# One K tile and one V tile of a cached attention step, loaded in three parts of 56, 64 and 8 partitions

## The chip, the cores and the metric

The kernel runs on one NeuronCore of a Trainium2 chip. The metric is the device time of one execution in microseconds (us). Profiles are of one execution, taken by the hardware profiler. The engines are called PE (TensorE, matmuls), PEld (its weight loads), DVE (VectorE), ACT (ScalarE), POOL (GpSimd) and SP (SyncE, which here only issues transfers). Transfers run on the core's 16 DMA engines, which are not in this list.

## The reference

One decode step of a transformer block for two sequences (B = 2, one new token each, D = 512), with 32 query heads, 8 K/V heads of 128 elements, and a cache of 32768 positions. All is float32. Cut to what matters:

```python
xn = layernorm(x)
q = (xn @ wq)                                   # 32 heads of 128
scores = einsum("bhqd,bhkd->bhqk", q, k) * 128 ** -0.5   # 4 query heads share a K/V head
o = einsum("bhqk,bhkd->bhqd", softmax(scores), v)
s = o.reshape(B, 1, 4096) @ wo
gate, up = xn @ W_gate, xn @ W_up
g = silu(((gate * (gate > 0)) * up) @ W_down)
out = x + s * g
```

The two caches are 2 x 8 x 32768 x 128 x 4 bytes = 268 MB each, and every byte is read once. The sum over positions in softmax and in the weighted sum of V doesn't depend on the order of the positions, as long as K and V are taken in the same order.

## The kernel before

The work is cut into 16 groups g, one for each sequence and K/V head, and each group into NU = 8 tiles of 4096 positions (`TK`). So there are 128 K tiles and 128 V tiles, numbered t = 0 to 127; tile t belongs to group t // 8. A tile is 2 MB: 128 partitions by 4096 floats, that is, each partition holds one row of 16 KB, which is 32 successive positions. `load_tile` makes one transfer of it, `rows` in device memory to `flat` in the tile, 128 rows of 16 KB (only V's last tile comes in two halves of the columns). All loads are issued on SP's queue, by `load`, in program order. Small loads of x (two rows each) are issued on ACT's queue at the start.

All big tiles live in one ring of `SLOTS = 8` buffers ("r"). A load can be issued when the buffer's last user is done: for a K tile that is the second of its two transposes on VectorE (`k_transpose`, line 298), for a V tile the last of its eight matmuls (`values`, line 383).

The main loop goes over steps s. In step s:

- VectorE transposes K tile s in 32 x 32 blocks, in two halves, into `kts` (line 298);
- PE multiplies it with the queries into `s` (`scores`, line 308), 16 matmuls;
- VectorE takes the scores of step s - 1 out of PSUM with their maximum (line 322);
- eight steps later, when the group's maximum is known, ACT has made the exponentials (line 359), PE and VectorE turn them (lines 365 and 374), and PE multiplies V tile v = s - 9 (`OFF = NU + LAG`) with them into `o_ps` (line 383).

When a group is done, its output is scaled and turned (`take_o`, `finish_group`), and after each K/V head PE multiplies with that head's rows of wo (`project_o`, line 434). The last head's wo rows (two transfers) are the last loads of the program, behind the two halves of the last V tile; the last matmuls on them, the product with the gate and the sum with x (lines 444 and 445) and two small stores (line 551) end the program. The MLP is done in the first steps.

Loads are issued `DEPTH = 3` steps ahead of their use: after step s, the table `ahead` has K tile s + 3 and V tile s + 3 - 9. So in steady state K and V loads alternate on SP, and tile k_64 and tile v_64 are 18 tiles apart in this order.

A load's completion is told by a semaphore. Loads take eight such semaphores (DMAHW0 to DMAHW7 in what follows) in turn, so a load uses the semaphore of the load eight issues before it and has to know that one landed.

Of the kernel before, what the change touches and what calls it, by code (L numbers as in the profile page):

```python
# [21 lines left out]
SLOTS = 8  # L22
DEPTH = 3
ALIGN = 512


@with_exitstack
def kernel(
# [18 lines left out]
    NU = SK // TK  # L47
    NG = B * HKV
# [34 lines left out]
    n = 1  # L83
# [41 lines left out]
    def load(dst, src):  # L125
        nc.sync.dma_start(dst, src)

    def group(g):
        return g % B, g // B

    def load_tile(dst, src, t, pieces):
        b, hk = group(t // NU)
        lo = (t % NU) * TK
        rows = src[b, hk, lo : lo + TK, :].rearrange("(p r) d -> p (r d)", p=P)
        flat = dst.rearrange("p c j d -> p (c j d)")
        c = 0
        for n in pieces:
            part = slice(c * NJ * DH, (c + n) * NJ * DH)
            load(flat[:, part], rows[:, part])
            c += n  # L140

    def load_k(t):
        KT[t] = ring.tile([P, NC, NJ, DH], F32, tag="r", align_bytes=ALIGN, name=f"k_{t}")
        load_tile(KT[t], kc, t, (NC,))

    def load_v(t):
        VT[t] = ring.tile([P, NC, NJ, DH], F32, tag="r", align_bytes=ALIGN, name=f"v_{t}")
        load_tile(VT[t], vc, t, (NC,) if t < NG * NU - 1 else LAST)

    def load_wo(hk):  # L150
        WO[hk] = ring.tile([P, 2, 2, D], F32, tag="r", align_bytes=ALIGN, name=f"wo_{hk}")
        r = REP * DH
        dst = WO[hk].rearrange("p c i d -> p c (i d)")
        rows = wo[hk * r : (hk + 1) * r, :].rearrange("(c p i) d -> p c (i d)", c=2, i=2)
        if hk < HKV - 1:
            load(dst, rows)
        else:
            for c in range(2):
                load(dst[:, c], rows[:, c])
# [5 lines left out]
    def load_wq(k):  # L165
        wqt[k] = ring.tile([P, 2, QW], F32, tag="r", align_bytes=ALIGN, name=f"wq_{k}")
        load(wqt[k].rearrange("p h n -> p (h n)"), wq[k * P : (k + 1) * P, :])
# [60 lines left out]
    def load_gu(which, half):  # L228
        t = ring.tile([P, 2, F], F32, tag="r", align_bytes=ALIGN, name=f"w{which}_{half}")
        w = wg if which == "g" else wu  # L230
        load(
            t.rearrange("p k f -> p (k f)"),
            w[half * 2 * P : (half + 1) * 2 * P, :].rearrange("(p k) f -> p (k f)", k=2),
        )
        for k in range(2):
            mlp[which, half * 2 + k] = t[:, k, :]
# [31 lines left out]
    def load_d(half):  # L268
        t = ring.tile([P, FH, D], F32, tag="r", align_bytes=ALIGN, name=f"wd_{half}")
        load(  # L270
            t.rearrange("p i d -> p (i d)"),
            wd.rearrange("(p i) d -> p (i d)", p=P)[:, half * FH * D : (half + 1) * FH * D],
        )
        for i in range(FH):
            mlp["d", half * FH + i] = t[:, i, :]
# [273 lines left out]
    rows = res.rearrange("(c q) n -> q c n", q=32)  # L549
# [33 lines left out]
```

## Time and profile before

| | |
|---|---|
| median of 3 runs | 1330.6 us (1330.4 to 1331.05) |
| the profiled execution | 1330.78 us |
| its span in the profile | 1328.9 us |
| DMA engines (queue q1, all loads of SP) | 99.5% of 16 engines' span, 564.68 MB |
| PE / DVE / ACT busy | 66% / 55% / 5% |
| a K load, from issue to landing | 28.4 us (median) |
| mean rate over the span | 426 GB/s |

The span is from the first to the last instruction of the profile; the profiled execution's time is 1.9 us longer. A DMA share is the mean share of time in which the 16 DMA engines had a packet in hand. Packets are the rows that a transfer moves (16 KB for a tile's row) and small ones of 4 bytes that close a transfer on an engine. "K from issue to landing" covers the wait in the engines' queues, since several loads are in flight at a time.

### The profile page before, as it was taken

To read this page: it belongs to the slowest core of one execution; us is meant where nothing else is said; L and a number is where in the kernel's file an instruction comes from. 1 tells how busy PE (TensorE), PEld (TensorE's weight loads), DVE (VectorE), ACT (ScalarE), POOL (GpSimd) and SP (SyncE) were. 2 spreads that over 40 slices of the span, in tenths; PEclk is the share of its full clock that TensorE was granted. 3 is DMA by queue.
4 is the path that set the end of the run, shared out by engine and by line. 5 is a ranking of instruction groups with operands and counts; after the bars stand their busy time and mean duration, and the time that the engine had idled before them with its cause. 6 is when DMAs were issued, how large, how long until landed. Compare 5 with 4: busy or idle time off the path is not lost.

```text
span 1328.9 us, 17052 instructions
## 1 busy us (share of the span) xinstructions
PE 872.7 (66%) x7544; PEld 338.5 (25%) x7544; DVE 727.7 (55%) x976; ACT 69.1 (5%) x261; POOL 0.7 (0%) x6
## 2 busy tenths in 40 slices
PE   4566675676666658566676766667676675767676
PEld 1232232232223223232222322223222231222222
DVE  5775555555645555554555555545555554646541
ACT  0001010100101000010100101000010100101010
POOL 0000000000000000000000000000000000000000
PEclk9778877888788887888887778878887787788888
DMA  9999999999999999999999999999999999999996
GB/s 397 430 430 431 430 429 431 430 430 430 430 431 429 431 431 430 429 430 431 429 431 428 431 431 430 431 429 431 431 428 431 429 431 431 429 431 430 431 431 288
DMA packets 40749, 565.77 MB, mean 426 GB/s; under 512 B 4434, under 2 KB 4450, under 8 KB 6500
## 3 DMA queue, kind: packets, MB, share of 16 engines
q1 hardware_dynamic: 40648, 564.68, 99.5%
q8 instruction: 59, 0.97, 0.3%
q14 instruction: 14, 0.11, 0.0%
q10 hardware_dynamic: 28, 0.01, 0.0%
HBM read 564.67 MB, written 0.00 MB: 425 GB/s over the span
## 4 chain that ended last, share of the span: by engine, by line
DMA 74%; DVE 14%; PE 11%; issue 0%; DVEq 0%
DMA k<-in_A_k_cache_dram 68%; DVE kts L298 12%; PE s L308 5%; PE o_ps L383 4%; DMA v<-in_A_v_cache_dram 2%; DMA wo<-in_A_wo_dram 2%; DMA wq<-in_A_wq_dram 2%; DVE sc L322 1%; PE pt L365 0%; DVE qt L220 0%; PE ps_u L242 0%; PE ps_d L281 0%; DVE os L406 0%; PE pq L198 0%; DVE boot L212 0%
## 5 line engine op out<-in xcount | busy, mean ns | idle before, releaser
L298 DVE STREAM_TRANSPOSE kts<-k 128x2048 f32<-128x2048 f32 x256 | 590.4, 2307 | 459.6 <-DMA k<-in_A_k_cache_dram 459.6
L308 PE MATMUL s<-kts,qt 128*32 128x256 f32 x4096 | 455.1, 526 | 326.5 <-DVE kts L298 322.5
L383 PE MATMUL o_ps<-v,sc 128*16 128x512 f32 (+1 forms) x2064 | 343.0, 685 | 6.2 <-DMA v<-in_A_v_cache_dram 6.1
L308 PEld LDWEIGHTS s<-kts,qt 128*32 128x32 f32 x4096 | 173.8, 141 | 556.5 <-issue 278.3
L383 PEld LDWEIGHTS o_ps<-v,sc 128*16 128x16 f32 (+1 forms) x2064 | 91.4, 115 | 149.6 <-issue 136.4
L359 ACT ACTIVATE sc<-sc,nb 128x256 f32<-128x256 f32 x128 | 63.2, 496 | 1126.4 <-DVE nb L355 1126.4
L374 DVE STREAM_TRANSPOSE sc<-pt 128x256 f32<-128x256 f32 x128 | 53.1, 415 | 82.4 <-PE pt L365 82.3
L365 PE MATMUL pt<-sc,perm 128*128 128x256 f32 x256 | 94.5, 453 | 0.9 <-ACT sc L359 0.9
L365 PEld LDWEIGHTS pt<-sc,perm 128*128 128x128 f32 x256 | 40.6, 199 | 112.4 <-issue 100.0
L322 DVE TENSOR_SCALAR_CACHE_REDUCE sc<-s 128x256 f32<-128x256 f32 x128 | 50.1, 392 | 5.9 <-PE s L308 5.5
L416 PE MATMUL po<-sel,os 128*64 128x4 f32 x512 | 25.0, 209 | 14.3 <-DVE os L406 14.3
L351 PE MATMUL pr<-negone,mrow 1*128 1x1 f32 x32 | 8.9, 344 | 37.5 <-DVE mrow L348 37.5
L336 PE MATMUL pr<-ident,m 128*1 128x128 f32 x16 | 4.6, 289 | 40.2 <-DVE m L334 40.2
L416 PEld LDWEIGHTS po<-sel,os 128*64 128x64 f32 x512 | 23.6, 147 | 20.8 <-DVE os L406 20.8
L359 ACT ACTIVATION_READ_ACCUMULATOR sc<-sc,nb 128x1 f32 x128 | 24.1, 188 | 0.0
L351 PEld LDWEIGHTS pr<-negone,mrow 1*128 1x128 f32 x32 | 7.5, 291 | 40.8 <-DVE mrow L348 40.8
L406 DVE TENSOR_SCALAR os<-o_ps,rl 128x512 f32<-128x512 f32 x16 | 12.0, 751 | 9.7 <-PE o_ps L383 8.5
L336 PEld LDWEIGHTS pr<-ident,m 128*1 128x1 f32 x16 | 1.3, 79 | 54.5 <-DVE m L334 53.6
L434 PE MATMUL py<-wo,ots 128*32 128x128 f32 x256 | 12.6, 313 | 0.1
L399 PE MATMUL pl<-l,same 128*128 128x1 f32 x32 | 6.7, 280 | 8.8 <-DVE l L397 8.8
L198 PE MATMUL pq<-wq,xnt 128*32 128x512 f32 x64 | 9.8, 769 | 2.7 <-DMA wq<-in_A_wq_dram 2.3
L434 PEld LDWEIGHTS py<-wo,ots 128*32 128x32 f32 x256 | 10.5, 131 | 2.0 <-issue 0.9
(69 smaller groups left out, 112.1 us busy)
## 6 DMA issues: line engine op xcount, KB each, us to landing
k<-in_A_k_cache_dram SPq DMA_DIRECT2D x128, 2048.0 KB, 28.4
v<-in_A_v_cache_dram SPq DMA_DIRECT2D x127, 2048.0 KB, 29.0
wq<-in_A_wq_dram SPq DMA_DIRECT2D x4, 2048.0 KB, 13.3
wo<-in_A_wo_dram SPq DMA_DIRECT2D x7, 1024.0 KB, 27.2
wg<-in_B_W_gate_dram SPq DMA_DIRECT2D x2, 1792.0 KB
wu<-in_B_W_up_dram SPq DMA_DIRECT2D x2, 1792.0 KB, 33.9
wd<-in_B_W_down_dram SPq DMA_DIRECT2D x2, 1792.0 KB
v<-in_A_v_cache_dram SPq DMA_DIRECT2D x2, 1024.0 KB
```

The lines of the kernel that those rows point to most:

```text
L198: nc.tensor.matmul(pq[half][32 * c : 32 * c + 32, :], xnt[:, k, :], wqt[k][:, half, c * 512 : (c + 1) * 512], start=(k == 0), stop=(k == N ...
L298: nc.vector.transpose(KTS[t][:, i * half : (i + 1) * half], src[:, i * half : (i + 1) * half])
L308: nc.tensor.matmul(ps[Q * c : Q * c + Q, :], qt[:, b, hk, e, :], mov[:, e, c], start=(e == 0), stop=(e == 3),)
L322: nc.vector.tensor_scalar(ST[t].rearrange("p j m -> p (j m)"), SPS.pop(t), SCALE, None, op0=ALU.mult, op1=ALU.max, accum_out=MX[g][:, u : ...
L351: nc.tensor.matmul(pr[:, 256:257], mrow.rearrange("o c k h -> o (c k h)"), negone, start=True, stop=True)
L359: nc.scalar.activation(st, st, AF.Exp, bias=nbias, scale=1.0, accum_out=LS[g][:, u : u + 1])
L365: nc.tensor.matmul(PW[t], perm.rearrange("p k c h -> p (k c h)"), ST[t].rearrange("p j m -> p (j m)"), start=True, stop=True,)
L374: nc.vector.transpose(ST[t].rearrange("p j m -> p (j m)"), PW.pop(t))
L383: nc.tensor.matmul(ops[g % 2][a : a + n * REP, :n, :], w[:, j, c * REP : (c + n) * REP], v[:, c : c + n, j, :], start=(u == 0 and j < 4), ...
L406: nc.vector.tensor_scalar(OS[g], ops[g % 2], rl, None, op0=ALU.mult)
L416: nc.tensor.matmul(pr[64 * r : 64 * r + 64, i * REP : (i + 1) * REP], o2[:, c, i, :], sel[:, c, :], start=(c == 0), stop=(c == NC - 1),)
L434: nc.tensor.matmul(py[32 * c : 32 * c + 32, :P], ots[:, hk % 2, k // 2, k % 2, :], w[:, k // 2, k % 2, c * P : (c + 1) * P], start=(hk == ...
```

## The change

Where tile t is 64 (`NG * NU // 2`), for K and for V, `load_tile` makes three transfers instead of one, of partitions 0 to 55, 56 to 119 and 120 to 127. In the first, the 56 source rows are taken as a 7 x 8 array, `(q a) -> a q` with a = 7: the seven values of a are the outer dimension, and partition 8a + q gets source row 7q + a. The other two keep the order of rows. The K tile and the V tile are permuted alike.

```diff
+PARTS = ((56, 7), (64, 0), (8, 0))
...
         flat = dst.rearrange("p c j d -> p (c j d)")
+        if t == NG * NU // 2:
+            p = 0
+            for n, a in PARTS:
+                part = rows[p : p + n, :]
+                load(flat[p : p + n, :], part.rearrange("(q a) f -> a q f", a=a) if a else part)
+                p += n
+            return
         c = 0
         for n in pieces:
```

In the built program four transfers more stand on SP's queue; the instructions of the other engines are the same. The place of k_64 on SP's queue, before (a row is the line, the operation, the tile and its source, partitions by elements, and what the issue waits for; PE_49 and DVE_49 are the semaphores of these engines, the number behind a tile's name is the buffer's):

```order
L126 DMA v_55_3013<-in_A_v_cache_dram 128x4096 [waits DMAHW2_49,DMAHW1_49,DVE_49]
L126 DMA k_64_3015<-in_A_k_cache_dram 128x4096 [waits PE_49]
L126 DMA v_56_3050<-in_A_v_cache_dram 128x4096 [waits DMAHW4_49,DMAHW3_49,DVE_49]
L126 DMA k_65_3052<-in_A_k_cache_dram 128x4096 [waits PE_49]
L126 DMA v_57_3087<-in_A_v_cache_dram 128x4096 [waits DMAHW6_49,DMAHW5_49,DVE_49]
```

Before, a V load's wait on two semaphores covers itself and the K load behind it. The same place after the change:

```order
L127 DMA v_55_3013<-in_A_v_cache_dram 128x4096 [waits DMAHW2_49,DMAHW1_49,DVE_49]
L127 DMA k_64_3015<-in_A_k_cache_dram 56x1x4096 [waits PE_49]
L127 DMA k_64_3015<-in_A_k_cache_dram 64x4096 [waits DMAHW3_49]
L127 DMA k_64_3015<-in_A_k_cache_dram 8x4096 [waits DMAHW4_49]
L127 DMA v_56_3052<-in_A_v_cache_dram 128x4096 [waits DMAHW5_49,DVE_49]
L127 DMA k_65_3054<-in_A_k_cache_dram 128x4096 [waits DMAHW6_49,PE_49]
L127 DMA v_57_3089<-in_A_v_cache_dram 128x4096 [waits DMAHW7_49,DVE_49]
```

The second and the third part wait for a semaphore of their own, and so does each of the next loads, up to k_67; since the tile took three semaphores, "eight issues before" is there the tile six places before instead of eight. The place of v_64 on SP's queue, before:

```order
L126 DMA wo_3_3363<-in_A_wo_dram 128x2x1024 [waits DMAHW4_49,DMAHW3_49,DVE_49]
L126 DMA v_64_3398<-in_A_v_cache_dram 128x4096 [waits PE_49]
L126 DMA k_73_3400<-in_A_k_cache_dram 128x4096 [waits DMAHW6_49,DMAHW5_49,DVE_49]
L126 DMA v_65_3435<-in_A_v_cache_dram 128x4096 [waits PE_49]
L126 DMA k_74_3437<-in_A_k_cache_dram 128x4096 [waits DMAHW7_49,DMAHW0_49,DVE_49]
```

And after:

```order
L127 DMA wo_3_3365<-in_A_wo_dram 128x2x1024 [waits DMAHW6_49,DMAHW5_49,DVE_49]
L127 DMA v_64_3400<-in_A_v_cache_dram 56x1x4096 [waits PE_49]
L127 DMA v_64_3400<-in_A_v_cache_dram 64x4096 [waits DMAHW7_49]
L127 DMA v_64_3400<-in_A_v_cache_dram 8x4096 [waits DMAHW0_49]
L127 DMA k_73_3404<-in_A_k_cache_dram 128x4096 [waits DMAHW1_49,DVE_49]
L127 DMA v_65_3439<-in_A_v_cache_dram 128x4096 [waits DMAHW2_49,PE_49]
L127 DMA k_74_3441<-in_A_k_cache_dram 128x4096 [waits DMAHW3_49,DVE_49]
```

Here too nothing is moved past anything else; the tile's one row became three, and the rows behind it wait one by one.

## The prediction

> **What bounds the kernel now.** I read the page's totals first, then its chain of waits and its idle times, then the DMA engines' share of busy time over stretches, in the middle and at the end. From the page:
>
> ```profile
> span 1328.9 us, 17052 instructions
> DMA  9999999999999999999999999999999999999996
> q1 hardware_dynamic: 40648, 564.68, 99.5%
> q8 instruction: 59, 0.97, 0.3%
> q10 hardware_dynamic: 28, 0.01, 0.0%
> DMA 74%; DVE 14%; PE 11%; issue 0%; DVEq 0%
> L298 DVE STREAM_TRANSPOSE kts<-k 128x2048 f32<-128x2048 f32 x256 | 590.4, 2307 | 459.6 <-DMA k<-in_A_k_cache_dram 459.6
> ```
>
> The sixteen DMA engines are busy in every slice but the last. The chain that ended last is 74% DMA, and VectorE, first to touch a K tile, stood idle 459.6 us for K tiles. So time is DMA time: 564.68 MB are 34,466 rows of 16 KB, which took 0.995 x 16 x 1328.9 = 21,156 us of engine time, **0.61 us a row on one engine**. A whole load is 128 rows, 8 on each engine, 4.9 us.
>
> Whether all engines end together is told by stretches at the end of the span (length, busy time of the five engine rows with counts, granted clock, mean DMA share, GB/s):
>
> ```profile
> 680.00:720.00 40.00, 26.07 (x200) 9.01 (x200) 21.86 (x21) 0.00 (x0) 0.00 (x0) 0.79 1.01 431
> 1311.00:1312.00 1.00, 1.00 (x12) 0.01 (x3) 0.00 (x0) 0.00 (x0) 0.00 (x0) 0.52 0.91 381
> 1312.00:1313.00 1.00, 1.00 (x5) 0.38 (x2) 0.00 (x0) 0.00 (x0) 0.00 (x0) 0.50 0.84 352
> 1313.00:1314.00 1.00, 0.84 (x2) 0.12 (x1) 0.12 (x1) 0.00 (x0) 0.00 (x0) 0.50 0.72 303
> 1314.00:1315.00 1.00, 0.12 (x4) 0.15 (x8) 0.38 (x2) 0.00 (x0) 0.00 (x0) 0.50 0.55 233
> 1317.00:1318.00 1.00, 1.00 (x8) 0.00 (x0) 0.00 (x0) 0.00 (x0) 0.00 (x0) 0.56 0.51 213
> 1321.00:1322.00 1.00, 0.44 (x10) 0.44 (x11) 0.51 (x1) 0.00 (x0) 0.00 (x0) 1.00 0.52 213
> 1322.00:1323.00 1.00, 1.00 (x32) 0.98 (x32) 0.00 (x0) 0.00 (x0) 0.00 (x0) 1.00 0.36 135
> 1323.00:1324.00 1.00, 1.00 (x41) 1.00 (x44) 0.33 (x2) 0.00 (x0) 0.00 (x0) 1.00 0.12 49
> 1324.00:1325.00 1.00, 0.92 (x36) 0.58 (x24) 0.00 (x0) 0.00 (x0) 0.00 (x0) 1.00 0.02 8
> ```
>
> This is the finding on which all hangs. Between 1311 and 1315 the share falls from 1 to 0.55, which is nine engines of sixteen (0.56): **seven engines have nothing left**. One more stops (0.51 is eight), six more at about 1322.6, and two (0.125) work until about 1324.2. The seven end at 1312.8 on average: the share above 0.56 in the first three of these rows sums to 0.79, and 0.79 / 0.44 is 1.8 us after 1311. I take 1314.2 for the last of them. So the seven are about 10 us ahead of the eight, though every load gives each engine equal rows. The page's q8 row fits: 59 packets of 16 KB of instructions, 0.3% of 16 x 1328.9 = 64 us of engine time, would be 7 us each if nine engines carried them. Also to be seen: with half the engines gone, those left move 213 GB/s at a share of 0.51, 26 GB/s each, against 431 / 16 = 27 before. An engine does not speed up when others stop; no common pool limits it.
>
> How the end hangs on them is told by the chain's last pieces (start, length, what):
>
> ```profile
> 1300.06 24.45 DMA wo<-in_A_wo_dram
> 1324.56 0.69 PE py L434 x16
> ```
>
> The last wo load lands with the last engine, at 1324.51; from there 16 matmuls, two VectorE operations and the store end the span. What moves the latest engine moves the end one to one.
>
> **The change, part by part.** K tile 64 and V tile 64 are loaded in 56 + 64 + 8 rows instead of 128, same bytes; both tiles' first 56 rows are permuted alike, so scores and values still meet, and no compute instruction is added or moved. Three costs remain: SP's queue, the engines' shares of rows, and the paths that the rows take.
>
> *SP's queue.* Four more issues. Rows of SP's time line, of the waits in 600 to 760 us, of K's landings there, and of the store, an issue of the longer kind:
>
> ```profile
> 622.47 0.33 SPq L126 DMA_DIRECT2D k<-in_A_k_cache_dram  x1
> 625.80 0.33 SPq L126 DMA_DIRECT2D v<-in_A_v_cache_dram  x1
> SPq L126 <- PE o_ps L383: 77.3, 16, 7.9
> DMA to landing us min/median/max: 27.4/28.5/30.2
> 1325.91 0.65 SPq L551 DMA_DIRECT2D out_dram<-res  x1
> ```
>
> 4 x 0.33 to 0.65 = 1.3 to 2.6 us on an engine that waits 77.3 us in this stretch for PE to free tiles. The order adds waits: k_64's second and third part, and each load behind them up to k_67, first wait for the load eight issues back, which is now about six tiles back. Behind a waiting part stand all later loads, v_56 first, and VectorE behind those. Six tiles are 6 x 4.9 = 29.3 us, landing takes 28.5 and at most 30.2, so a load may be issued up to 1 us late. The cover is the 28 us of work that stands in each engine's queue; SP's part costs nothing until that is used up, and then what is late is the next K tile, us for us.
>
> *Shares of rows.* No load on SP before shows fewer than 16 engines, but ACT's small ones do:
>
> ```profile
> xy<-in_A_x_dram ACTq DMA_DIRECT2D x4, 1.0 KB
> boot<-in_A_x_dram ACTq DMA_DIRECT2D x1, 4.0 KB
> out_dram<-res ACTq DMA_DIRECT2D x1, 2.0 KB
> ```
>
> They move 4 x 2 + 2 + 4 = 14 rows, and q10 has 28 packets: 14 more, as many as there are rows, where one closing packet on each of 16 engines would have made 96 more. So a load runs on as many engines as its outer dimension has steps. The parts' source has 7, 64 and 8 outer steps: 7 engines with 8 rows, 16 with 4, 8 with 1. If each count starts at the same engine, seven engines get 13 rows a tile, one 5 and eight 4, instead of 8. Over both tiles: seven engines +10 rows = **+6.1 us**, one -6 rows = -3.7 us, eight -8 rows = **-4.9 us**. That is 7, 1 and 8 engines, the very groups in which the last stretches empty, so I take the seven that gain rows to be the seven that end early. [...]
>
> With rows alone: the seven end at 1314.2 + 6.1 = 1320.3 at the latest, the eight at 1324.2 - 4.9 = 1319.3: the end comes 1324.2 - 1320.3 = 3.9 us earlier.
>
> *The paths.* In a whole load each engine fills its own eight partitions, again and again. The parts give that up: seven engines fill 56 neighbouring partitions, then sixteen fill the next 64 in fours, then eight the last 8. If the 27 GB/s belong to the way into a group of partitions and not to the engine, two engines that meet on one way take turns. No row before shows two engines on one way. Bounds: nothing at the low end (a gain is excluded, since no engine ever ran faster than 27 GB/s), and at the high end each of the 13 rows a tile takes twice 0.61 us: 26 x 0.61 = 15.9 us. The nearest rows are those of 1317 to 1322: engines freed of company stay at 26 to 27, so the limit is private to an engine and its way, and that leaves both ends open. I take a value near the high end, 12 of 13 rows doubled (all but the single row of the last part), 24 x 0.61 = 14.6 us, because the seven run almost in step (they ended within some 3 us, five rows, of each other) and so keep meeting for most of an eight-row block. The engines hit are the seven, on average at 1312.8 + 6.1 + 14.6 = 1333.5 instead of an end at 1324.2: **+9.3 us**. The high end, on the last of the seven, is 1314.2 + 6.1 + 15.9 = 1336.2, +12.0 us. The eight lose time too where they meet the seven, but have 4.9 us and the seven's lateness as cover.
>
> [...]
>
> **Sum.** Profiled execution 1330.78 us (its span 1328.9; the median of the runs is 1330.6, 0.2 lower) + 6.1 + 14.6 on the seven, less the 11.4 us (1324.2 - 1312.8) that they have in hand = 1340.1; I say **1340.0**.
>
> **The rivals.**
> 1. *The rows only level the engines* (not slower): no turn-taking. The seven idle engines and the matching groups speak for it; against it only that the paths are no longer each engine's own. 1330.8 - 3.9 = 1326.9. Between it and the forecast the point that decides is 5.3 us of turn-taking (11.4 - 6.1), some 9 of the 26 rows at half speed.
> 2. *The seven that get more rows are not the seven that idle*: no row names engines. An engine that ends at 1324.2 gets +6.1: 1336.9 even without turn-taking.
> 3. *The change does not do what it says, or cancels*: the parts are spread over all engines after all, or turn-taking is about 5 us and eats the gain: 1330.8.
>
> **Chances.** Forecast 0.55, rival 1 0.28, rival 2 0.07, rival 3 0.10. A measurement of this kernel tells 0.2% (2.7 us) from no change: slower is 0.55 + 0.07 = 0.62, faster 0.28, same 0.10. The forecast's own range is 1335 (four rows in ten spared) to 1343 (the high end). Without rival 1 more than two in ten would be left out, so the range reaches to its time, 1326.4 to 1343.
>
> **What the profile after would show.** Forecast: around 640 to 660 and 735 to 755 the DMA share stays near 1 while GB/s falls, as rows take longer than 0.61 us; k_64 and v_64 land 5 us or more later than 28.5; at the end the picture is turned round, nine engines gone first and a share near 0.44 for about 10 us. Rival 1: GB/s stays at 430 in the middle, and the share stays over 0.9 until about 1317. Rival 2: the last stretch has few engines, and a longer one than before. Wrong altogether would be a new wait on SP for landings of more than 1 us a time, with the DMA share dropping in mid-kernel: then the queues ran dry, which I priced at nothing.

## The result and the profile after

The changed kernel takes 1364.15 us (median; 1362.1 to 1368.3), the one before, run beside it, 1331.05: a ratio of 1.0253 with a 95% interval of 1.0239 to 1.0268. It is 33.1 us slower; 9.3 us had been forecast, and the range ended at 1343.

The page of the changed kernel, its rates in 40 slices of 34 us and its queue q1:

```profile
GB/s 397 429 429 432 431 429 431 429 430 431 429 430 430 430 431 431 430 430 378 309 431 360 310 430 430 431 429 429 430 430 430 429 430 431 429 431 430 430 431 236
q1 hardware_dynamic: 40678, 564.68, 99.2%
```

Before, all slices but the first (397) and the last (288) show 428 to 431. Now two places fall to 309 and 310, and the last slice to 236; elsewhere nothing has changed. The bytes are the same, and q1 has 30 packets more than the 40648 of before: 2 x (7 + 16 + 8 - 16), as parts that run on 7, 16 and 8 engines would make.

The two places, in windows of 10 us (the columns behind the length are PE, PEld, DVE, ACT and POOL, each with a count, then the granted clock, the DMA share and GB/s):

```profile
630.00:640.00 10.00, 6.63 (x56) 2.47 (x50) 5.19 (x5) 0.00 (x0) 0.00 (x0) 0.83 1.06 415
640.00:650.00 10.00, 5.48 (x50) 2.10 (x48) 5.19 (x5) 0.00 (x0) 0.00 (x0) 0.83 0.99 210
650.00:660.00 10.00, 1.25 (x10) 0.10 (x2) 0.00 (x0) 0.00 (x0) 0.00 (x0) 0.79 1.00 182
660.00:670.00 10.00, 0.37 (x1) 0.08 (x1) 4.07 (x5) 0.00 (x0) 0.00 (x0) 0.50 0.98 326
...
730.00:740.00 10.00, 6.73 (x54) 2.46 (x58) 5.51 (x7) 0.00 (x0) 0.00 (x0) 0.83 1.03 357
740.00:750.00 10.00, 3.49 (x44) 1.20 (x37) 0.13 (x1) 0.00 (x0) 0.00 (x0) 0.90 1.03 256
750.00:760.00 10.00, 4.22 (x35) 1.96 (x35) 5.66 (x11) 2.97 (x13) 0.00 (x0) 0.50 1.01 203
760.00:770.00 10.00, 4.31 (x26) 1.46 (x22) 0.49 (x2) 1.07 (x5) 0.00 (x0) 0.84 0.97 259
```

The kernel before, at the first place:

```profile
640.00:650.00 10.00, 6.63 (x55) 2.45 (x50) 5.19 (x5) 0.00 (x0) 0.00 (x0) 0.83 1.00 429
650.00:660.00 10.00, 5.21 (x43) 2.26 (x37) 5.66 (x11) 3.48 (x15) 0.00 (x0) 0.83 1.01 429
```

The share stays at 1: no engine ran out of rows, each row took longer. Against 430 GB/s the first four windows lost 13.7 us (15 + 220 + 248 + 104 = 587, times 10 us / 430) and the last four 15.0 us. These 28.7 us are most of the 33.1. At 182 GB/s more than the seven engines must be slow: nine undisturbed engines would move 9 x 27 (430 / 16) = 243 alone. The trace also has the start and duration of every packet, and these show that it is all sixteen: of the 297 rows of 16 KB that start between 639.5 and 664 us, none takes less than 0.96 us, and the median is 1.25; before, 640 of the 641 in the same stretch take 0.61. PE and VectorE (the first and the third of the columns) have less to do in these windows. The end of the span:

```profile
1340.00:1345.00 5.00, 2.67 (x22) 0.72 (x18) 0.92 (x3) 0.00 (x0) 0.00 (x0) 1.00 0.82 342
1345.00:1350.00 5.00, 2.69 (x18) 0.85 (x18) 0.49 (x2) 0.00 (x0) 0.00 (x0) 0.87 0.42 175
1350.00:1355.00 5.00, 4.11 (x43) 1.20 (x35) 0.92 (x2) 0.00 (x0) 0.00 (x0) 0.79 0.18 75
1355.00:1360.00 5.00, 3.52 (x96) 2.96 (x96) 0.91 (x4) 0.00 (x0) 0.00 (x0) 1.00 0.06 21
```

A share of 0.18 is three engines of sixteen, of 0.06 one. So it is not seven engines that end last, as forecast, but a few. The rest of the 33.1 us, 4.4 us, is here. The chain's last load:

```profile
1333.54 24.45 DMA wo<-in_A_wo_dram
```

It lands at 1357.99, 33.5 us later than the 1324.51 of before.

### The profile page after: what moved, and what is told of

Its sections match the earlier page's. It is cut to its first block, busy times and chain, and to the rows that moved or that the text cites. A ratio compares the mean times of both kernels' runs of the same rounds, so it can differ in the third digit from the quotient of the medians.

```text
span 1362.3 us, 17064 instructions
## 1 busy us (share of the span) xinstructions
PE 869.0 (64%) x7544; PEld 342.0 (25%) x7544; DVE 727.7 (53%) x976; ACT 69.1 (5%) x261; POOL 0.7 (0%) x6
## 4 chain that ended last, share of the span: by engine, by line
DMA 76%; DVE 14%; PE 10%; issue 0%; DVEq 0%; SPq 0%
DMA k<-in_A_k_cache_dram 70%; DVE kts L306 11%; PE s L316 5%; PE o_ps L391 4%; DMA v<-in_A_v_cache_dram 2%; DMA wo<-in_A_wo_dram 2%; DMA wq<-in_A_wq_dram 2%; DVE sc L330 1%; DVE qt L228 1%; DVE boot L220 0%; PE ps_d L289 0%; PE ps_g L250 0%; PE pt L373 0%; DVE os L414 0%; PE pr L359 0%
## 5 line engine op out<-in xcount | busy, mean ns | idle before, releaser
L391 PE MATMUL o_ps<-v,sc 128*16 128x512 f32 (+1 forms) x2064 | 338.9, 678 | 5.6 <-DMA v<-in_A_v_cache_dram 5.6
L442 PEld LDWEIGHTS py<-wo,ots 128*32 128x32 f32 x256 | 10.5, 135 | 2.1 <-issue 1.1
```

Of the source, the lines that this page charges most:

```text
L391: nc.tensor.matmul(ops[g % 2][a : a + n * REP, :n, :], w[:, j, c * REP : (c + n) * REP], v[:, c : c + n, j, :], start=(u == 0 and j < 4), ...
L442: nc.tensor.matmul(py[32 * c : 32 * c + 32, :P], ots[:, hk % 2, k // 2, k % 2, :], w[:, k // 2, k % 2, c * P : (c + 1) * P], start=(hk == ...
```

## The experiments

Each run stands against the kernel before, timed beside it (1330.6 to 1331.7 us).

**Four more loads alone.** From the kernel before: the two tiles in three pieces of columns, so that each piece still has 128 partitions.

```diff
+        if t == NG * NU // 2:
+            pieces = (2, 1, 1)
```

> K tile 64 and V tile 64 in three loads again, but cut by columns: each load has all 128 partitions, of 8, 4 and 4 KB a row. So there are as many loads, semaphores and waits on SP as in the change, every engine keeps its 8 rows a load and its own partitions. If the number of loads and SP's waits for landings cost the 33 us: about 1360 us. If the ways into the partitions or the unequal rows do it: 1331 us, within 1 us of the kernel before, and 430 GB/s throughout.

1330.66 us, ratio 0.9996 (0.9986 to 1.0005). The additional issues, semaphores and waits on SP cost nothing that can be told.

**Two halves.** The change with `PARTS = ((64, 0), (64, 0))`: sixteen engines with 4 rows in each half, so 8 rows a tile as before, in plain order.

> K tile 64 and V tile 64 in two halves of 64 partitions, rows in order: 16 engines with 4 rows each in each half, so every engine keeps 8 rows a tile, but sixteen engines write into 64 partitions at a time. If unequal rows or the row order of the first part cost the time: 1331 us. If two engines on one way take fair turns: a half takes twice its 2.4 us, +2.4 us a half, 4 halves, +9.8 us, 1341 us, rows of about 1.2 us. If the blocked ways hold up everybody, as the rate of 180 to 210 GB/s over 26 to 30 us in the changed kernel suggests: more than fair turns, 1345 to 1360 us.

1351.73 us, ratio 1.0156 (1.0141 to 1.0171). The windows behind k_64:

```profile
640.00:650.00 10.00, 4.80 (x38) 1.90 (x42) 5.19 (x5) 0.00 (x0) 0.00 (x0) 0.68 0.99 215
650.00:660.00 10.00, 1.91 (x14) 0.21 (x6) 0.00 (x0) 0.00 (x0) 0.00 (x0) 0.84 1.01 213
```

Equal rows and no new order, yet half the rate for 20 us at a share of 1. Of the 269 rows of 16 KB that start between 639.5 and 660 us none takes less than 0.91 us, the median 1.2. Neither the shares of rows nor the 7 x 8 order is needed for the loss.

**Even and odd partitions.** Again two parts of 64 rows on sixteen engines:

```diff
+        if t == NG * NU // 2:
+            load(flat[0::2, :], rows[0::2, :])
+            load(flat[1::2, :], rows[1::2, :])
+            return
```

> k_64 and v_64 are each loaded in two parts of 64 rows, as in the run with halves, but the first part is the even partitions and the second the odd ones. Every engine then gets 4 rows of each part, and they lie in the eight partitions that it fills in a whole load. Theory (what costs is a row that an engine writes into partitions that belong to another engine's whole loads): no such row is left, 1330.7 within 1 us, GB/s stays at 430. Rival (a tile in parts of fewer partitions costs, whichever they are): as the halves, about 1351.7, GB/s near 215 for some 21 us behind k_64.

1331.27 us, ratio 1.0002 (0.9993 to 1.0011), and the same windows:

```profile
640.00:650.00 10.00, 5.48 (x42) 2.03 (x46) 5.25 (x6) 0.00 (x0) 0.00 (x0) 0.67 1.00 429
650.00:660.00 10.00, 6.00 (x46) 2.42 (x39) 5.60 (x11) 3.56 (x15) 0.00 (x0) 0.67 1.00 428
```

Number of parts, rows for each and engines are those of the halves; only which partitions a part fills differs. That decides 20 us. Which engine fills which of the even partitions no run shows.

**Which partitions: seven engines.** For this and what follows, the kernel before gets loads in addition, into a scratch tile that nothing reads, at K tiles 48, 56, 64 and 72:

```diff
+    scratch = const.tile([P, 2048], F32, name="scratch")
...
+        if t in (48, 56, 64, 72) and src is kc:
+            for i, p in enumerate((0, 32)):
+                part = rows[28 * i : 28 * i + 28, :2048].rearrange("(q a) f -> a q f", a=7)
+                load(scratch[p : p + 28, :], part)
```

The next kernel differs from this only in `(64, 96)` for `(0, 32)`, and a third one has the change's first part alone, with half rows: `load(scratch[:56, :], rows[:56, :2048].rearrange("(q a) f -> a q f", a=7))`. All three put 8 half rows on each of seven engines at each tile.

> The kernel before with eight extra loads: at K tiles 48, 56, 64 and 72, 28 rows of 8 KB (7 outer steps of 4 rows, so seven engines) into partitions 0 to 27 and again into 32 to 59 of a scratch tile that nothing reads. [...] Each adds 8 half rows, 2.4 us, to seven engines, 9.8 us in all. If the seven are the ones that end 10 us early and nothing blocks: 1331 to 1332 us, and the DMA share at the end falls for fewer engines. If any load on seven engines, or the interleaved source rows, slow everybody: 4 stretches of low GB/s and 1345 us or more. If the seven are not the idle ones: 1341 us.

> The same eight extra loads, same source rows, sizes and seven engines, but into partitions 64 to 91 and 96 to 119 and up to 123, which other engines fill in a whole load. If the ways into the partitions are what costs: GB/s falls in four stretches, and the time is at least 10 us (fair turns: 4 x 2.4 us on the blocked engines) over that of the extra loads into partitions 0 to 27 and 32 to 59. If the ways do not matter: the same time as that one within 1 us.

> The kernel before plus, at K tiles 48, 56, 64 and 72, one extra load of 56 rows of 8 KB, taken as 7 x 8, into partitions 0 to 55: the change's first part alone. Seven engines write 8 half rows each into the partitions that they fill in a whole load. If it costs only the rows: GB/s stays at 430 and the time is that of the two loads of 28 rows, about 1339.5 (4 x 8 x 0.31 = 9.9 us on late engines). If it holds up others by itself, as the 2 x 8 load into partitions 0 to 15 did a little (404 and 388 GB/s for 6 us): GB/s falls under 410 at the four places and the time is 1342 or more.

Partitions 0 to 27 and 32 to 59: 1339.31 us (ratio 1.0063, 1.0048 to 1.0078). Partitions 64 to 91 and 96 to 123: 1364.66 (1.0252, 1.0224 to 1.028). Partitions 0 to 55: 1351.44 (1.0169, 1.0140 to 1.0197). Behind the first of the four tiles, the first kernel, the second, the third:

```profile
481.00:484.00 3.00, 0.62 (x4) 0.17 (x4) 3.00 (x4) 0.00 (x0) 0.00 (x0) 1.00 1.01 431
484.00:487.00 3.00, 1.17 (x13) 0.59 (x16) 2.12 (x2) 0.00 (x0) 0.00 (x0) 0.54 1.01 431
```

```profile
480.00:490.00 10.00, 6.48 (x57) 2.30 (x50) 5.19 (x5) 0.00 (x0) 0.00 (x0) 0.83 1.04 261
```

```profile
481.00:484.00 3.00, 1.25 (x6) 0.39 (x6) 3.00 (x4) 0.00 (x0) 0.00 (x0) 1.00 1.07 350
484.00:487.00 3.00, 1.32 (x16) 0.69 (x20) 1.96 (x2) 0.00 (x0) 0.00 (x0) 0.80 0.97 265
```

The third run was the surprise. Its expectation took partitions 8e to 8e + 7 to be what engine e fills in a whole load; then the change's first part would disturb nobody. It loses 13.0 us of rate over the four tiles (slices of the page, worked out as above), while the first kernel, whose seven engines (a = 0 to 6) fill 4a to 4a + 3 and 32 + 4a to 32 + 4a + 3, loses none; every one of its rows of 16 KB that starts between 480 and 490 us takes 0.61 us. I take the latter to be what these engines fill in a whole load too. The three runs agree with it (431, 261 and, with partitions 0 to 55, 350 and 265 GB/s), but no trace names the partitions that an engine fills.

The undisturbed first kernel is 8.7 us slower all the same, and its end tells why:

```profile
1324.00:1326.00 2.00, 2.00 (x12) 0.22 (x4) 0.00 (x0) 0.00 (x0) 0.00 (x0) 0.50 0.19 78
1326.00:1328.00 2.00, 1.99 (x22) 0.88 (x18) 0.17 (x1) 0.00 (x0) 0.00 (x0) 0.67 0.19 80
1328.00:1330.00 2.00, 1.10 (x17) 0.39 (x17) 0.75 (x1) 0.00 (x0) 0.00 (x0) 1.00 0.17 72
```

Three engines (0.19 of sixteen) work on alone for some 8 us; their rows in addition are 4 x 8 x 0.31 = 9.9 us (the rows of 8 KB of V's last tile take 0.31 us in the kernel before). Three of the seven engines that got rows are among the late ones.

**Which partitions: two engines.** `load(scratch[64:80, :], rows[:16, :2048].rearrange("(q a) f -> a q f", a=2))` at the same tiles, then `scratch[0:16, :]`, then `scratch[32:48, :]`. Two engines write 8 half rows each.

> The kernel before plus, at the same four K tiles, one extra load of 16 rows of 8 KB, taken as 2 x 8, into partitions 64 to 79: two engines write 8 rows each into the partitions of two others. Work alone: 2.5 us each time on two engines, 9.9 us in all; the end at 1331 to 1341 according to whether these two are early or late ones; GB/s stays at 430. Fair turns: four engines of sixteen at half speed for 5 us each time, GB/s about 376 there, the end at 1340 to 1350. Theory (foreign rows hold up all sixteen): GB/s falls well under 376 at each place, rows of all sixteen engines take over 0.61 us, and by the price of the earlier run (6.3 us / 56 rows) each time costs all engines 1.8 us.

> The extra loads of 16 rows of 8 KB, taken as 2 x 8, at K tiles 48, 56, 64 and 72, into partitions 0 to 15, which the two engines fill in a whole load. GB/s stays at 430. If these two are of the seven that end early, their 9.9 us of rows fill about what they have in hand: 1330.6 to 1332. If they are late ones: 1340.5.

> The extra loads of 16 rows of 8 KB, taken as 2 x 8, again at K tiles 48, 56, 64 and 72, but into partitions 32 to 47 instead of 64 to 79. If each engine's eight partitions are a way of its own, two engines again write into those of two others: GB/s falls to about 280 for 4.5 us at each place and the time is near 1339.4. [...]

Into 64 to 79: 1339.39 us (1.0060, 1.0045 to 1.0075). Into 0 to 15: 1342.76 (1.0093, 1.0075 to 1.0111). Into 32 to 47: 1342.34 (1.0082, 1.0067 to 1.0097). Windows in this order:

```profile
481.00:484.00 3.00, 1.58 (x8) 0.47 (x6) 3.00 (x4) 0.00 (x0) 0.00 (x0) 1.00 1.06 279
484.00:487.00 3.00, 1.37 (x20) 0.83 (x24) 1.91 (x2) 0.00 (x0) 0.00 (x0) 0.89 0.97 303
```

```profile
481.00:484.00 3.00, 1.45 (x8) 0.47 (x6) 3.00 (x4) 0.00 (x0) 0.00 (x0) 1.00 0.99 404
484.00:487.00 3.00, 1.26 (x16) 0.72 (x20) 2.02 (x2) 0.00 (x0) 0.00 (x0) 0.85 1.01 388
1325.00:1330.00 5.00, 4.37 (x30) 1.29 (x34) 0.17 (x1) 0.00 (x0) 0.00 (x0) 0.66 0.13 55
1330.00:1335.00 5.00, 4.13 (x104) 2.92 (x96) 1.08 (x3) 0.00 (x0) 0.00 (x0) 1.00 0.09 31
```

```profile
481.00:484.00 3.00, 0.62 (x4) 0.17 (x4) 3.00 (x4) 0.00 (x0) 0.00 (x0) 0.96 1.00 407
484.00:487.00 3.00, 1.33 (x16) 0.64 (x20) 1.95 (x2) 0.00 (x0) 0.00 (x0) 0.50 0.96 382
1325.00:1330.00 5.00, 3.65 (x22) 1.04 (x26) 0.00 (x0) 0.00 (x0) 0.00 (x0) 0.69 0.10 43
1330.00:1335.00 5.00, 4.09 (x85) 2.50 (x88) 1.25 (x4) 0.00 (x0) 0.00 (x0) 0.97 0.08 30
```

Two readings. First, the two writers into 64 to 79 slow all sixteen engines, not only those they meet: of the 37 rows of 16 KB that start between 482 and 485.3 us none takes less than 0.99 us, the median 1.16. Second, 0 to 15 and 32 to 47 give nearly the same pictures and times (404 and 388 against 407 and 382 GB/s, 1342.76 against 1342.34 us), another than 64 to 79 (279 and 303 GB/s). 32 to 47 did not fall to about 280. For 0 to 15 the expected 430 GB/s did not come in either, nor 1330.6 to 1332 us, though it had 1340.5 as its other branch, for late engines: if an engine's own partitions are the two fours taken above, the two engines stay in their own for half of one engine's rows only. So, on that reading, a row in another engine's partitions does not always bring the full price: here 60 of 95 rows (0 to 15) and 71 of 97 (32 to 47) that start between 481.9 and 486 us take less than 0.64 us, and at each of the first three places well under 1 us is lost. At the fourth the slice loses 3.5 and 2.7 us, and there the share falls too (to 0.69 from 754 to 760 us with 0 to 15), so engines had no rows to move. Why the rate falls so little in these two, and one or two engines end 5 to 10 us behind the others, is not settled.

**The other parts, and where they stand.** 64 half rows into partitions 56 to 119 (`load(scratch[56:120, :], rows[:64, :2048])`) at the four tiles, the same at K tiles 4, 12, 20, 28 and at 96, 104, 112, 120; 8 half rows into partitions 120 to 127; and the first part with the 64 rows right behind it.

> The kernel before plus, at K tiles 48, 56, 64 and 72, one extra load of 64 rows of 8 KB into a scratch tile's partitions 56 to 119: the change's second part alone, with half-length rows. 4 rows of 0.31 us an engine, 1.24 us each time: if only the work counts, 1330.6 + 4.9 = 1335.5. Fair turns (eight ways for sixteen engines): 2.5 us each time, 1340.6. Theory (foreign rows hold up all sixteen): the extra loads into partitions 64 to 91 and 96 to 123 cost 6.3 us for each 56 rows, so some 7 us each time, 1359, with GB/s at 240 for about 12 us at each of the four places.

> The extra loads of 64 rows of 8 KB into partitions 56 to 119, at K tiles 4, 12, 20 and 28 instead of 48, 56, 64 and 72. There the engines finish a load within 1 to 2 us of each other, where at tiles 48 to 72 it is 4.7 to 6.1 us. Theory (everything runs at half speed from the first engine's first foreign row to the last engine's last one, so the price grows with how far the engines are out of step): some 3 us each time, about 1343. Rival (the price belongs to the rows, wherever they stand): 1357 as before.

> The same extra loads at K tiles 96, 104, 112 and 120, where the engines finish a load within 8.9 to 10.3 us of each other. Theory (price grows with the spread): 9 to 10 us each time, about 1368. Rival (price by rows): 1357.

> The kernel before plus, at the same four K tiles, one extra load of 8 rows of 8 KB into partitions 120 to 127: the change's third part alone. Eight engines get one row each, all into the eight partitions of one engine. Only the work: 4 x 0.31 = 1.2 us, 1331.9. By the theory at the price per row of the earlier run (6.3 us / 56 rows): 0.9 us each time, 1334.2. If the one way takes the eight rows in turn and everything stands behind it: 2.5 us each time, 1340.5.

> At the same four tiles, the 56 rows as 7 x 8 into partitions 0 to 55 and right behind them 64 rows into partitions 56 to 119. If the first part only adds its rows: the sum of the two runs, 1331 + 26.3 + 9 = 1366, with the losses of GB/s at the four places as with the 64 rows alone (4.6 us each time). If the first part makes the block behind it longer: over 6 us lost each time, 1372 or more.

The 64 rows: 1356.93 us (ratio 1.0196, 1.0179 to 1.0213); early 1350.53 (1.0146, 1.0128 to 1.0164); late 1360.69 (1.0229, 1.0212 to 1.0246). The 8 rows: 1335.98 (1.0038, 1.0024 to 1.0051). Both long parts: 1374.94 (1.0342, 1.0315 to 1.0368). The slices of the 64 rows, early and late, then of the first part alone and of both:

```profile
GB/s 397 408 431 395 429 429 388 429 385 423 431 430 429 429 432 430 430 431 430 429 431 430 429 430 432 429 429 431 431 429 430 432 429 429 432 429 430 431 430 284
```

```profile
GB/s 397 431 429 430 430 430 431 429 430 432 429 428 432 430 429 431 430 429 431 430 431 429 429 429 432 427 432 431 368 431 380 405 431 366 429 400 383 430 430 279
```

```profile
GB/s 398 430 429 431 430 431 429 430 430 430 430 430 429 431 397 429 390 429 431 383 430 399 415 430 430 430 429 431 431 429 431 430 426 431 429 430 431 429 432 253
```

```profile
GB/s 397 431 429 431 430 429 432 429 430 430 430 430 429 431 339 431 345 426 430 325 429 385 371 430 429 431 430 431 430 430 430 430 428 431 429 431 428 431 429 241
```

What a slice lacks of 430, as a share of 430 and times its length of about 34 us, is lost time: at each of the four tiles 3.0 us early and 5.5 late, and 4.6 at tiles 48 to 72. In the kernel before, the sixteen engines land a load within 1.9 to 3.5 us of each other at the early tiles, 4.7 to 6.4 at 48 to 72 and 8.9 to 10.5 at the late ones. So the price goes up with how far the engines are out of step, early as expected (some 3 us), late less (9 to 10 us had been expected). That the spread is the reason is argued from three places in the kernel, not shown. The early run stands 7 us above its 1343; some 5 of them are the extra rows' own time on each engine (4 x 4 x 0.31), which that figure leaves out. The first part alone loses 3.3 us each time, both parts 7.8, about 3.3 + 4.6: the prices add. The 8 rows lose 0.7 us each time.

**The order within the first part, and of the parts.** The change with `PARTS = ((56, 0), (64, 0), (8, 0))`, so the first part is 14 x 4, and the change with the 7 x 8 part issued last:

```diff
+            for p, n, a in ((56, 64, 0), (120, 8, 0), (0, 56, 7)):
+                part = rows[p : p + n, :]
+                load(flat[p : p + n, :], part.rearrange("(q a) f -> a q f", a=a) if a else part)
```

> The change with its first part in plain row order: 56 rows as 14 x 4 instead of 7 x 8. Then fourteen engines write 4 rows each, nearly all into partitions of others, where the seven wrote 8 rows each into their own. The engines' rows a tile come to 9, 8 and 4 instead of 13, 5 and 4. Theory (rows in others' partitions are what costs): the two long parts block as the halves did (+21 us), the last parts add some 3, the uneven rows some 1: about 1356, with GB/s near 215 for longer at k_64 than in the change. Rival (the seven chunks in another order are what costs, and the 13 rows on seven engines): without them 1331 to 1340.

> The change with its three parts issued in another order: partitions 56 to 119 first, then 120 to 127, then the 7 x 8 part. Every engine has the same rows in the same partitions as in the change. Theory (the block lasts from the first engine's foreign row to the last engine's, and in the change the 7 x 8 part holds seven engines back by 8 x 0.61 = 4.9 us ahead of it): the losses at k_64 and v_64 shrink from 13 and 15 us to about the 10.5 of the plain 14 x 4 parts, 1364.2 - 7 = 1357. Rival (the seven's 13 rows, or the 7 x 8 part itself, are the cost): no change, 1364.

14 x 4: 1353.06 us (1.0162, 1.0147 to 1.0177). The 7 x 8 part last: 1363.10 (1.0241, 1.0226 to 1.0256). So 7 x 8 costs 10 to 11 us more than 14 x 4, first or last; the theory that it costs by holding seven engines back ahead of the 64 rows fell.

## Why the prediction was wrong

The direction and the kind of cost were right: rows take longer (1.25 us instead of 0.61) where parts leave what I take to be the engines' own partitions, the rate falls while the share stays at 1, and the time comes out longer. By its steps:

- *SP's queue costs nothing*: held, shown by the column pieces (1330.66).
- *7, 16 and 8 engines, so +10, -6 and -8 rows*: the numbers of engines held (30 packets).
- *"I take the seven that gain rows to be the seven that end early"*: failed. Three of them are late ones, as the end of the run with partitions 0 to 27 and 32 to 59 showed, so their rows (+6.1 us) count at the end instead of in the 11.4 us in hand. This was rival 2, with a chance of 0.07, and it came true together with the forecast's slower rows.
- *The first part's rows meet others too* (12 of 13 rows doubled): the side of it that can be seen held; that part alone lost 3.3 us each time. That each engine's own eight partitions are eight neighbours was taken only in expectations of runs, and failed (350 and 265 GB/s with partitions 0 to 55).
- *The paths, 0 to 15.9 us on the seven*: this is the step on which the forecast failed: the term was mis-sized, and the bound itself was wrong. I priced it as two engines taking turns, with the others as cover ("the eight ... have 4.9 us and the seven's lateness as cover"). The runs showed that the hold-up spreads to all sixteen engines, whose rows take twice as long: the whole stream of loads lost 28.7 us at the two tiles, against 14.6 us on seven engines. And what all engines lose can't be taken out of the 11.4 us that some of them have in hand. The halves show it purest: no engine has a row more, and it costs 21.1 us.
- *"No common pool limits it"*, from the last stretch of before: that row shows that an engine left alone goes no faster (26 GB/s against 27). Only whole loads run there, so it could say nothing of parts.

With the measured 28.7 us and the 6.1 us of rows, the sum is 1330.8 + 28.7 + 6.1 = 1365.6 against 1364.15. At the end 4.4 us more were measured than before, so the 6.1 is some 1.5 us too much.

The trace shows 1.25 us a row on all engines instead of 0.61; by what way the hold-up reaches engines that meet nobody was not measured.

Open: why the first part as 7 x 8 costs 10 to 11 us more than as 14 x 4. Some 4 to 5 us of it stand in the last slice (236 against 292 GB/s), where the late engines' rows count; the rest is at the two tiles. The busiest engine has 13 rows a tile against 9, but that was not tried alone. Open as well is why the two extra loads into 0 to 15 and 32 to 47 disturbed so little.

## What to carry to other kernels

Where loads bound a kernel, cut a tile by columns, or into even and odd partitions, which cost nothing here, and not into halves of 64 neighbouring partitions, which cost 21.1 us for two tiles. Of the blocks of neighbouring partitions only 0 to 27 with 32 to 59 left the rate alone (431 GB/s), which I take to be what their engines fill in whole loads. Before pricing contention, ask not only who meets whom but who waits behind them: a bound that holds for the engines that collide says nothing about the rest. And an even split of work over engines says nothing about which of them end late.

## What the hardware showed unexpectedly

Sixteen half rows (0.13 MB) written by two of sixteen engines into partitions 64 to 79 bring the whole core's loads from 430 to 279 and then 303 GB/s for some 6 us, with about 2 us lost and the rows of all sixteen engines at 1.0 to 1.3 us; into 0 to 15 or 32 to 47 the rate stays at 382 to 407. And 56 half rows by seven engines into partitions 0 to 27 and 32 to 59 leave 431 GB/s. Two parts of 64 neighbouring partitions run at 214 GB/s for 20 us; two parts of every second partition at 429.
